# Scores of two heads in nearly every place with the values beside them, and the weights' conversion weighted to the places with values

## The chip, the core and the metric

The kernel runs on one core of a Trainium2 chip. The metric is the device time of one execution in microseconds (us). PE is TensorE (its matmuls; PEld is its weight loads), DVE is VectorE, ACT is ScalarE, POOL is GpSimd and SP is SyncE, which here only issues DMAs. Each engine runs its own instructions strictly in the order in which they were issued; a semaphore holds an instruction back until its inputs are there.

## What is computed

Attention of 8 batches, 12 heads, 448 tokens and head size 64, with the heads mixed before and after the softmax, and behind it a two-layer feed-forward block on the 3584 tokens. All is float32.

```python
def _attn_ref(q, k, v, w_pre, w_post):
    scale = 1.0 / np.sqrt(q.shape[-1])
    scores = scale * np.matmul(q, k.transpose(0, 1, 3, 2))
    scores = np.einsum('bhij,hg->bgij', scores, w_pre)
    scores = scores - np.max(scores, axis=-1, keepdims=True)
    attn = np.exp(scores)
    attn = attn / (np.sum(attn, axis=-1, keepdims=True) + 1e-09)
    attn = np.einsum('bhij,hg->bgij', attn, w_post)
    return np.matmul(attn, v)

def _moe_ref(x, w_in, w_out):          # x: [3584, 768]
    h = x @ w_in                       # d_ff = 2048
    return (h - np.tanh(h)) @ w_out
```

## The kernel before, in words

**Stages.** A start of some 26 us, an attention loop (26 to 838 us), and the feed-forward stage (to 1787 us). The change touches only the attention loop.

**Places.** The 448 query rows of a batch are cut into blocks of 120, 120, 120 and 88 rows, 32 blocks in all. A block is split into groups of up to ten query rows times twelve heads (120 partitions), 360 groups; two groups make a *place*, and the loop `for p in range(NPL + 3)` runs over NPL = 180 places. At each place PE does `premix(p)` (L521: the mixing before the softmax, into the two banks `ps_p`), then the jobs that a table `todo[p]` gives it, then `mix(p - 1)` (L560: the mixing behind the softmax of the place before, into `ps_o`). A place needs, from the others:

- `expo(p)`: on DVE two maxima (L530), on ACT two exponentials with their sums (L532);
- `norm(p - 1)`, issued ahead of `expo(p)`: on DVE the reciprocal of the sums (L541, L542), on POOL the scaled weights `wr` (L543) that `mix(p - 1)` multiplies by;
- the copy of `mix`'s result out of `ps_o` into the block's tile `at` on ACT (L570, or L577 in two parts where a place spans two blocks). It is issued at the start of the next place, and `ps_o` has one buffer, so `mix(p)` also waits for the copy of `mix(p - 1)`;
- `gather`: DMAs that bring the scores of the next groups into `t` (L510, issued by SP).

**Jobs.** `scores(i, hp)` makes the scores of one pair of heads for block i: 6 matmuls (L477) into two banks of `ps_m`, copied to the tile `s` by ACT (one bank) and DVE (the other), both L482. `values(i, t)` is half of attention times V for block i: 24 matmuls (L602) into one bank, copied to `x` by DVE (L620). `prep_q` and `prep_k` transpose Q (L443) and K (L417) into one bank per call; ACT makes the high part (L456, L428), DVE the low part (L458, L429). `ps_m` has four banks in turn. In the trace a plain float32 matmul stands twice, so `values` shows as x48 there, and `scores` of one pair as x6.

**Order within a place.** The queues on ACT and DVE follow the calls: first `mixed()` (the copy into `at`), `norm`, `expo`, then, after PE's jobs, the copies of K, Q and scores (list `sooner`), then `conv.place()`, and only then the low parts (list `then`) and the copy of the values into `x` (list `last`).

**The conversion.** Beside all this the feed-forward weights are turned into two float32 parts and written to DRAM (`narrow_chunk`): 56 chunks of 384 or 512 columns, each 11 steps with 5 operations on DVE (L80, L83, L87, L89, L94), 3 on ACT (L82, L85, L102), 3 on POOL (L96, L98, L104) and DMAs. `Steps` deals the steps out evenly, 617 steps over 164 places, 3.76 per place; what is left is done by `conv.rest(now)` at place 177, ahead of the first loads of the next stage.

**The planner.** What sets `todo` is a small scheduler ahead of the loop: each block has due places for its scores (three jobs of two pairs, four heads each) and its values (two halves), and one job goes to one place, scores and values in turn where both are ready.

Of the kernel before, what the change touches and what calls it, by code (L numbers as in the profile page):

```python
# [37 lines left out]
def narrow_steps(nc, pool, dma, chunks):  # L38

    def load(src):
        p, n2 = src.shape
        r = pool.tile([p, CW, 2], I32, name="cr", tag="cr", bufs=3)[:, : n2 // 2]
        return r, dma(r.rearrange("p n t -> p (n t)"), src)


    todo, loads, active = list(chunks), [], []  # L50
    yield
    while todo or loads or active:
        while todo and len(loads) + len(active) < 3:
            src, dst = todo.pop(0)
            loads.append((*load(src), dst))
        while loads and len(active) < 2:
            r, landed, dst = loads[0]
            if not landed(1):
                break
            loads.pop(0)  # L60
            active.append(narrow_chunk(nc, pool, dma, r, dst))
        for it in list(active):
            if next(it, "end") == "end":
                active.remove(it)
            else:
                yield
        if not active:
            yield


def narrow_chunk(nc, pool, dma, r, dst):
    p, n, _ = r.shape
    hi, lo = r[:, :, 1], r[:, :, 0]
    m = pool.tile([p, CW], F32, name="cm", tag="cm", bufs=2)[:, :n]
    s = pool.tile([p, CW], I32, name="cs", tag="cs", bufs=2)[:, :n]
    u, w = hi, lo

# [11 lines left out]
    nc.vector.scalar_tensor_tensor(  # L89
        out=u, in0=m.bitcast(I32), scalar=3, in1=s, op0=ALU.logical_shift_left, op1=ALU.bitwise_or  # L90
    )
    yield "step"

    nc.vector.tensor_scalar(s, u, -(2**23), None, op0=ALU.bitwise_and)  # L94
# [3 lines left out]
    nc.gpsimd.tensor_tensor(out=m, in0=m, in1=u.bitcast(F32), op=ALU.add)  # L98
# [12 lines left out]


class Steps:


    def __init__(self, it, steps, places):
        self.it = it
        self.rate = steps / places
        self.due = 0.0

    def place(self):
        self.due += self.rate
        while self.due >= 1.0:
            self.due -= 1.0
            next(self.it, None)
# [23 lines left out]
def kernel_body(  # L149
# [11 lines left out]
    nc = tc.nc  # L161
# [4 lines left out]
    NP = H // 2  # L166
# [9 lines left out]
    NM = len(sizes)  # L176
# [162 lines left out]
    with ExitStack() as st:  # L339
# [4 lines left out]
        cv = early.enter_context(tc.tile_pool(name="cv", bufs=1, side="left"))  # L344
# [11 lines left out]
        blocks = [(b, m) for b in range(B) for m in range(NM)]  # L356
# [3 lines left out]
        queue, slow, sent = [], [], {}  # L360
# [41 lines left out]
        KB = 4  # L402
# [336 lines left out]
        NG = len(groups)  # L739
# [2 lines left out]
        place[0] += 1  # L742
        scores_of(1, 0)
        NPL = NG // 2
        conv = Steps(narrow_steps(nc, cv, partial(dma, to=slow), chunks), 11 * len(chunks) + 1, NPL - 16)

# [9 lines left out]
        halved = []  # L756
        for i in range(len(blocks)):

            f0, f1, f2 = first[i : i + 3]
            if i + 1 < len(blocks):  # L760
                lo = max(0, (f0 - 1) // 2 - 1)
                hi = f1 // 2 - 3
# [3 lines left out]
            for x in range(2):  # L766
                halved.append(((f1 - 1) // 2 + 2, f2 // 2 + 1 if f2 < NG else NPL + 7, "v", i, x))
        at_s, p, kind = {}, 0, None
        while halved:
            ready = sorted((x for x in halved if x[0] <= p), key=lambda x: (x[1], x[3:]))  # L770
            if ready:
                x = ready[0]
                assert p <= x[1], (p, x)

                other = [y for y in ready if y[2] != kind]
                if x[2] == kind and other and x[1] > p + 1:
                    x = other[0]
                halved.remove(x)
                _, _, kind, i, n = x
                if kind == "s":  # L780
                    at_s[i, n] = p
                    for hp in (2 * n, 2 * n + 1):
                        at_place(p, scores, i, hp)
                else:
                    at_place(p, values, i, n)
            p += 1
        for i, (b, m) in enumerate(blocks):
            p0 = first[i] // 2
            if i + 2 < len(blocks):
                p = at_s[i + 2, 0] - 1  # L790
                at_place(p, prep_q, i + 2, 0)
                at_place(p, prep_q, i + 2, 1)
                if i + 3 < len(blocks):
                    at_place(p + 1, load_q, i + 3)
            if b and m == 0:
                for hq in range(NP // 2):
                    at_place(p0 + 4 + hq, load_v, b, hq)
        for b in range(1, B):
            p, o, done = first[blocks.index((b - 1, 1))] // 2 - 4, 0, []
            for hq in range(3):  # L800
                if hq == 2:

                    p = max(p, done[0] + 1)
                at_place(p, load_k, b, hq)
                o = max(p + 4, o + 1)
                p += 1
                if hq > KB - 4:

                    o = max(o, at_s[blocks.index((b - 1, 3)), hq - 1 - (KB - 4)] + 1)
# [5 lines left out]
                assert o < at_s[blocks.index((b, 0)), hq], (b, hq)  # L815

        rank = {prep_k: 0, prep_q: 0, values: 1, scores: 2}
        for x in todo.values():
            x.sort(key=lambda job: rank.get(job[0], 3))

        def hidden_0():
            ff.r = next(gate(hidden(0)))
# [60 lines left out]
    for n in range(N):  # L883
        b, f = n // NF, n % NF
# [63 lines left out]
```

## Time and profile before

Three runs took 1787.08 to 1787.36 us, the median 1787.1. The profiled execution took 1788.92 us, of which the profile's span is 1787.2 us; the 1.7 us between them lie around the program.

| | busy us | share of span | instructions |
|---|---|---|---|
| PE matmuls | 1751.0 | 98% | 16572 |
| DVE | 1128.3 | 63% | 2362 |
| ACT | 1000.5 | 56% | 2051 |
| POOL | 320.1 | 18% | 417 |

"Busy" for PE includes matmuls that overlap each other, and the ends of matmuls are modelled. Shares are averages over two stages with different limits; the table of windows that the next part quotes looks at the attention loop and at single places.

### The profile page before, as it was taken

The numbers are of one execution on the slowest core, as the hardware profiler recorded it, in microseconds if no ns is written. First come the engines' busy times: TensorE is split into PE (matmuls) and PEld (weight loads), VectorE is DVE, ScalarE is ACT, GpSimd is POOL, SyncE is SP. The second block draws the span as 40 slices with busy tenths as digits, with TensorE's granted clock in tenths as the row PEclk, the third lists the DMA queues.
The fourth block names the chain that finished last, engine by engine and source line by source line (L and its number), as shares of the span: only waits on it lengthen the run. The fifth ranks groups of instructions, "written<-read, shape, count | busy, mean of one in ns | idle before, by whom it ended". The sixth has DMA issues, their size and how long they took to land.

```text
span 1787.2 us, 41382 instructions
## 1 busy us (share of the span) xinstructions
PE 1751.0 (98%) x16572; PEld 1425.6 (80%) x16572; DVE 1128.3 (63%) x2362; ACT 1000.5 (56%) x2051; POOL 320.1 (18%) x417
## 2 busy tenths in 40 slices
PE   8999999999999999999999999999999999999998
PEld 6777777777777777777888888888888888888887
DVE  5676777777777767664556566565565565655555
ACT  5777877777777776765343443433434434444333
POOL 1333333333333333321010010000000000000000
PEclk9999999999999999999999999999999999999999
DMA  8668687777967687565655655655656655655651
GB/s 176 204 196 216 194 236 224 217 215 215 249 203 218 215 213 220 178 202 216 255 207 194 248 193 207 241 193 214 229 197 216 224 208 204 228 217 190 230 194 36
DMA packets 232816, 372.32 MB, mean 208 GB/s; under 512 B 98992, under 2 KB 207536, under 8 KB 218288
## 3 DMA queue, kind: packets, MB, share of 16 engines
q1 hardware_dynamic: 231740, 368.45, 64.0%
q8 instruction: 131, 2.15, 0.5%
q10 hardware_dynamic: 884, 1.22, 0.2%
q14 instruction: 61, 0.50, 0.1%
HBM read 245.37 MB, written 47.19 MB: 164 GB/s over the span
## 4 chain that ended last, share of the span: by engine, by line
PE 87%; DMA 4%; ACT 4%; DVE 3%; issue 1%; POOL 0%; SPq 0%; ACTq 0%; DVEq 0%; POOLq 0%
PE ps_o L560 13%; PE ps_h L257 8%; PE ps_h L258 8%; PE ps_h L262 8%; PE ps_m L602 8%; PE ps_p L521 7%; PE ya L305 6%; PE ya L302 6%; PE ya L303 6%; PE ps_q L477 5%; PE yb L305 3%; PE yb L303 3%; PE yb L302 3%; DMA t<-s 2%; PE ps_m L443 1%
## 5 line engine op out<-in xcount | busy, mean ns | idle before, releaser
L560 PEld LDWEIGHTS ps_o<-wr,e 60*112 60x112 f32 (+1 forms) x5760 | 306.2, 176 | 44.3 <-POOL wr L543 21.8
L560 PE MATMUL ps_o<-wr,e 60*112 60x60 f32 (+1 forms) x5760 | 315.5, 259 | 14.3 <-POOL wr L543 7.7
L530 DVE TENSOR_REDUCE mx<-ps_p 128x1 f32<-128x448 f32 x360 | 207.7, 619 | 163.9 <-PE ps_p L521 163.7
L532 ACT ACTIVATE e<-ps_p,mx 128x448 f32<-128x448 f32 x360 | 225.7, 634 | 101.9 <-DVE mx L530 99.4
L289 ACT CAST gh<-r 128x512 fp32r<-128x512 f32 x112 | 69.6, 621 | 372.6 <-DVE r L282 372.6
L258 PE MATMUL ps_h<-xl,w 128*128 128x512 f32 x672 | 264.4, 393 | 0.0
L257 PE MATMUL ps_h<-xh,w 128*128 128x512 f32 x672 | 264.3, 393 | 0.0
L570 ACT COPY at<-ps_o 112x960 f32<-112x960 f32 x156 | 153.7, 985 | 93.8 <-PE ps_o L560 93.2
L247 POOL TENSOR_TENSOR xl<-rx,xh 128x512 fp32r<-128x512 f32 x38 | 55.6, 1464 | 731.2 <-ACT xh L246 731.2
L521 PE MATMUL ps_p<-t,wpre 60*64 60x448 f32 (+1 forms) x1440 | 180.8, 569 | 3.9 <-DMA t<-s 2.7
L305 PE MATMUL ya<-w,gl 128*128 128x512 f32 x448 | 177.0, 395 | 0.7 <-DVE gl L290 0.7
L278 DVE SCALAR_TENSOR_TENSOR r<-qa,ps_h 128x512 f32<-128x512 f32 x112 | 77.1, 688 | 159.2 <-ACT t L275 159.2
L302 PE MATMUL ya<-w,gh 128*128 128x512 f32 x448 | 174.8, 390 | 1.0 <-ACT gh L289 1.0
L303 PE MATMUL ya<-w,gh 128*128 128x512 f32 x448 | 174.8, 390 | 0.0
L602 PEld LDWEIGHTS ps_m<-at,vr 112*64 112x64 f32 x3072 | 147.5, 137 | 31.0 <-ACT at L577 10.9
L262 PE MATMUL ps_h<-xh,w 128*128 128x512 f32 x672 | 170.6, 389 | 0.0
L602 PE MATMUL ps_m<-at,vr 112*64 112x120 f32 (+1 forms) x3072 | 161.6, 261 | 8.4 <-ACT at L577 3.1
L272 ACT ACTIVATE u<-ps_h 128x512 f32<-128x512 f32 x112 | 67.0, 599 | 152.9 <-PE ps_h L262 152.9
L262 PEld LDWEIGHTS ps_h<-xh,w 128*128 128x128 f32 x672 | 126.3, 188 | 26.3
L258 PEld LDWEIGHTS ps_h<-xl,w 128*128 128x128 f32 x672 | 127.5, 190 | 23.7
L257 PEld LDWEIGHTS ps_h<-xh,w 128*128 128x128 f32 x672 | 127.4, 190 | 23.4
L543 POOL TENSOR_TENSOR wr<-wpost,zs 128x120 f32<-128x120 f32 x180 | 70.2, 390 | 402.9 <-DVE zs L542 293.6
(93 smaller groups left out, 3038.0 us busy)
## 6 DMA issues: line engine op xcount, KB each, us to landing
w<-ws SPq DMA_DIRECT2D x112, 1536.0 KB
t<-s SPq DMA_DIRECT2D x342, 210.0 KB
cr<-in_moe_w_in_dram SPq DMA_DIRECT2D x24, 512.0 KB
cr<-in_moe_w_out_dram SPq DMA_DIRECT2D x32, 384.0 KB
vr<-in_v_dram SPq DMA_DIRECT2D x24, 448.0 KB
kr<-in_k_dram SPq DMA_DIRECT2D x23, 448.0 KB
out_dram<-ob SPq DMA_DIRECT2D x24, 384.0 KB
qr<-in_q_dram SPq DMA_DIRECT2D x23, 360.0 KB
```

What stands on the lines that cost most here:

```text
L257: nc.tensor.matmul(ph, wh[:, fs], xh, start=(c == 0), stop=False)
L258: nc.tensor.matmul(ph, wh[:, fs], xl, start=False, stop=False)
L262: nc.tensor.matmul(ph, wl[:, fs], xh, start=False, stop=(c == NK - 1))
L302: nc.tensor.matmul(y, gh[:, tok], wh[:, es], start=first, stop=False)
L303: nc.tensor.matmul(y, gh[:, tok], wl[:, es], start=False, stop=False)
L305: nc.tensor.matmul(y, gl[:, tok], wh[:, es], start=False, stop=last)
L521: nc.tensor.matmul(pss[r][halves[j], :], wpre[k, :], ts[j][k, :], start=True, stop=True)
L530: nc.vector.tensor_reduce(out=mx, in_=ps, axis=AX.X, op=ALU.max, negate=True)
L532: nc.scalar.activation(e, ps, AF.Exp, bias=mx, scale=1.0, accum_out=zs[:, 0, r : r + 1])
L560: nc.tensor.matmul(ps[:CP, j, c * GP : (c + 1) * GP].rearrange("p (h i) -> p h i", i=GI)[:, :, r * GH : (r + 1) * GH], e[k, c * CP : (c + ...
L570: nc.scalar.copy(ats[i0][:, :, :, at : at + 2 * GI].rearrange("p c h (j i) -> p j (c h) i", j=2), ps[:CP, :, : NC * GP].rearrange("p j (x ...
L602: nc.tensor.matmul(pv[j * D : (j + 1) * D, r, :n], vt[:, j, c, :], ats[i][:, c, 2 * hp + j, :n], start=(c == 0), stop=(c == NC - 1),)
```

## The change

The table `todo` is made by other rules. Scores are dealt out pair by pair (two heads), evenly over the places at which a block's scores may run, so that most places get one pair. Values go to the first place from their due place on that has at most one pair, if the last values lie two places back. The transposes go where a place's jobs need no more than four banks in all; the two halves of `prep_q` are at two places where they can be. V is loaded only once the values of the block before are placed, and the first values of a batch are due two places later. `Steps` takes a list of weights, 2.5 for a place with values and 1 for another, over the same 164 places.

```diff
 class Steps:
-    def __init__(self, it, steps, places):
+    def __init__(self, it, steps, weights):
         self.it = it
-        self.rate = steps / places
+        self.rates = [steps * w / sum(weights) for w in weights]
         self.due = 0.0
     def place(self):
-        self.due += self.rate
+        self.due += self.rates.pop(0) if self.rates else 0.0
...
-                for x in range(0 if i else 1, 3):
-                    e = lo + 2 * x if lo + 4 <= hi else lo + (hi - lo) * x // 2
-                    halved.append((e if i else x - 1, hi, "s", i + 1, x))
+                due_s += [(lo, hi, i + 1, hp) for hp in range(0 if i else 2, NP)]
+            lo = (f1 - 1) // 2 + (4 if i and i % NM == 0 else 2)
+            due_v += [(lo, f2 // 2 + 1 if f2 < NG else NPL + 7, i, x) for x in range(2)]
...
+                left = sum(x[2] == i for x in due_s)
+                now_s = -(-left // (hi - p + 1))
...
+                if p + (1 - x) >= hi or now_s == 0 or now_s == 1 and apart >= 2:
+                    due_v.pop(0)
+                    at_place(p, values, i, x)
...
+                p = max(p0 + 4, at_v[i - 1, 1] + 1)
                 for hq in range(NP // 2):
-                    at_place(p0 + 4 + hq, load_v, b, hq)
+                    at_place(p + hq, load_v, b, hq)
...
-                    while any(f is scores or f is prep_q for f, *a in todo[o]):
+                    while banks(o) > 3:
...
+        weight = [2.5 if any(f is values for f, *a in todo[p]) else 1 for p in range(4, NPL - 12)]
+        conv = Steps(narrow_steps(nc, cv, partial(dma, to=slow), chunks), 11 * len(chunks) + 1, weight)
         rank = {prep_k: 0, prep_q: 0, values: 1, scores: 2}
```

The number of instructions of each kind stays. The places come out so (of 179, with the transposes left out of the count):

| jobs of the place | before | after |
|---|---|---|
| four heads' scores | 92 | 26 |
| one pair's scores (two heads) | 0 | 88 |
| values alone | 62 | 18 |
| values and one pair's scores | 0 | 44 |
| neither | 25 | 3 |

How it moves the rows is shown at places 42 and 43. First PE, before; a place begins with its premix (L521), and `ps_q` are the scores' banks:

```order
L521 MATMUL ps_p<-t,wpre 64x448 x4
L477 MATMUL ps_q<-kk,qh 120x448 x4
L477 MATMUL ps_q<-kk,ql 120x448 x2
L477 MATMUL ps_q<-kk,qh 120x448 x4
L477 MATMUL ps_q<-kk,ql 120x448 x2
L560 MATMUL ps_o<-wr,e 112x12x5 x16
L521 MATMUL ps_p<-t,wpre 64x448 x4
L443 MATMUL ps_m<-ident,qr 128x120 x6
L602 MATMUL ps_m<-at,vr 64x120 x24
L560 MATMUL ps_o<-wr,e 112x12x5 x16
```

The same two places on PE after the change:

```order
L521 MATMUL ps_p<-t,wpre 64x448 x4
L443 MATMUL ps_m<-ident,qr 128x120 x3
L602 MATMUL ps_m<-at,vr 64x120 x24
L477 MATMUL ps_q<-kk,qh 120x448 x4
L477 MATMUL ps_q<-kk,ql 120x448 x2
L560 MATMUL ps_o<-wr,e 112x12x5 x16
L521 MATMUL ps_p<-t,wpre 64x448 x4
L477 MATMUL ps_q<-kk,qh 120x448 x4
L477 MATMUL ps_q<-kk,ql 120x448 x2
L560 MATMUL ps_o<-wr,e 112x12x5 x16
```

The values now have a pair's scores behind them in the same place, and the next place has only one pair between its premix and its mix.

DVE at the same two places, before (a place's rows begin with the maxima, L530, and end with the reciprocal, L542, that the next mix needs; `cm`, `cr` and `cs` belong to the conversion):

```order
L530 TENSOR_REDUCE mx<-ps_p 128x1 x2
L482 COPY s<-ps_q 120x448 x2
L89 SCALAR_TENSOR_TENSOR cr<-cm,cs 128x384
L94 TENSOR_SCALAR cs<-cr 128x384
L541 TENSOR_SCALAR zs<-zs 128x1 x2
L542 RECIPROCAL zs<-zs 128x2
L530 TENSOR_REDUCE mx<-ps_p 128x1 x2
L80 TENSOR_SCALAR cm<-cr 128x384
L458 SCALAR_TENSOR_TENSOR ql<-ps_m,qh 128x3x120 x2
L620 COPY x<-ps_m 128x3x12x10
L541 TENSOR_SCALAR zs<-zs 128x1 x2
L542 RECIPROCAL zs<-zs 128x2
```

And DVE after the change, place 42 whole and the first rows of place 43:

```order
L530 TENSOR_REDUCE mx<-ps_p 128x1 x2
L482 COPY s<-ps_q 120x448
L87 TENSOR_SCALAR cs<-cr 128x384
L89 SCALAR_TENSOR_TENSOR cr<-cm,cs 128x384
L94 TENSOR_SCALAR cs<-cr 128x384
L458 SCALAR_TENSOR_TENSOR ql<-ps_m,qh 128x3x120
L620 COPY x<-ps_m 128x3x12x10
L541 TENSOR_SCALAR zs<-zs 128x1 x2
L542 RECIPROCAL zs<-zs 128x2
L530 TENSOR_REDUCE mx<-ps_p 128x1 x2
L482 COPY s<-ps_q 120x448
```

In the place with values the copy of the scores now stands first behind the maxima, and three operations of the conversion, the low part of Q, the copy of the values and the reciprocal stand behind it.

Last, SP's queue of DMAs at the end of the loop. Before, the first load of the next stage's weights (`w`, L334) follows the last gathers:

```order
L510 DMA t<-s 120x1x448 x8
L369 DMA xs_64<-x 768x1x240
L510 DMA t<-s 120x1x448 x4
L510 DMA t<-s 108x1x448 x2
L334 DMA w_12920<-ws_65 128x3072
```

After the change:

```order
L510 DMA t<-s 120x1x448 x12
L369 DMA xs_64<-x 768x1x240
L510 DMA t<-s 120x1x448 x4
L510 DMA t<-s 108x1x448 x2
L369 DMA ws_68<-cs 128x384
L369 DMA ws_68<-cl 128x384
L334 DMA w_12920<-ws_65 128x3072
```

The last chunk of the conversion is finished by `conv.rest` at place 177, and its two writes stand ahead of that load.

More of the change, by code (lines that the diff above doesn't have):

```diff
@@ L754, in at_place, with banks @@
             todo[p].append(job)
-        halved = []
+        def banks(p):
+            return sum({scores: 2, values: 1, prep_q: 1, prep_k: 1}.get(f, 0) for f, *a in todo[p])
+        at_s, at_v = {}, {}
+        due_s, due_v = [], []
         for i in range(len(blocks)):
@@ L760, in kernel_body @@
             if i + 1 < len(blocks):
-                lo = max(0, (f0 - 1) // 2 - 1)
-                hi = f1 // 2 - 3
-                for x in range(0 if i else 1, 3):
-                    e = lo + 2 * x if lo + 4 <= hi else lo + (hi - lo) * x // 2
-                    halved.append((e if i else x - 1, hi, "s", i + 1, x))
[L766 to L785, printed above, removed]
+                lo, hi = max(0, (f0 - 1) // 2 - 1), f1 // 2 - 3
+                due_s += [(lo, hi, i + 1, hp) for hp in range(0 if i else 2, NP)]
+            lo = (f1 - 1) // 2 + (4 if i and i % NM == 0 else 2)
+            due_v += [(lo, f2 // 2 + 1 if f2 < NG else NPL + 7, i, x) for x in range(2)]
+        p, apart = 0, 2
+        while due_s or due_v:
+            now_s = 0
+            if due_s and due_s[0][0] <= p:
+                _, hi, i, _ = due_s[0]
+                left = sum(x[2] == i for x in due_s)
+                assert p <= hi, (p, hi, i)
+                now_s = -(-left // (hi - p + 1))
+                for _ in range(now_s):
+                    _, _, i, hp = due_s.pop(0)
+                    at_s[i, hp] = p
+                    at_place(p, scores, i, hp)
+            if due_v and due_v[0][0] <= p:
+                _, hi, i, x = due_v[0]
+                assert p <= hi, (p, hi, i)
+                if p + (1 - x) >= hi or now_s == 0 or now_s == 1 and apart >= 2:
+                    due_v.pop(0)
+                    at_v[i, x] = p
+                    at_place(p, values, i, x)
+                    apart = 0
+            apart += 1
             p += 1
@@ L788, in kernel_body @@
             p0 = first[i] // 2
[L789 to L794, printed above, removed]
             if b and m == 0:
+                p = max(p0 + 4, at_v[i - 1, 1] + 1)
+                assert p + 4 < at_v[i, 0], (p, at_v[i, 0])
                 for hq in range(NP // 2):
-                    at_place(p0 + 4 + hq, load_v, b, hq)
+                    at_place(p + hq, load_v, b, hq)
         for b in range(1, B):
@@ L807, in kernel_body @@
                 if hq > KB - 4:
-                    o = max(o, at_s[blocks.index((b - 1, 3)), hq - 1 - (KB - 4)] + 1)
+                    o = max(o, at_s[blocks.index((b - 1, 3)), 2 * (hq - 1 - (KB - 4)) + 1] + 1)
                 for r in range(2):
-                    while any(f is scores or f is prep_q for f, *a in todo[o]):
+                    while banks(o) > 3:
                         o += 1
@@ L814, in kernel_body @@
                 done.append(o)
-                assert o < at_s[blocks.index((b, 0)), hq], (b, hq)
+                assert o < at_s[blocks.index((b, 0)), 2 * hq], (b, hq)
+        last_q = 0
+        for i in range(len(blocks)):
+            if i + 2 < len(blocks):
+                p = at_s[i + 2, 0]
+                for t in (1, 0):
+                    p -= t
+                    while banks(p) > 3:
+                        p -= 1
+                    at_place(p, prep_q, i + 2, t)
+                    last_q = max(p, last_q) if t == 0 else p
+                assert p > at_s.get((i, NP - 1), 0), p
+                p = last_q
+                if i + 3 < len(blocks):
+                    at_place(p + 1, load_q, i + 3)
+        weight = [2.5 if any(f is values for f, *a in todo[p]) else 1 for p in range(4, NPL - 12)]
+        conv = Steps(narrow_steps(nc, cv, partial(dma, to=slow), chunks), 11 * len(chunks) + 1, weight)
         rank = {prep_k: 0, prep_q: 0, values: 1, scores: 2}
         for x in todo.values():
-            x.sort(key=lambda job: rank.get(job[0], 3))
+            x.sort(key=lambda job: (rank.get(job[0], 3), job[2] if job[0] is prep_q else 0))
         def hidden_0():
```

1 line of the change is left out of this document (removed).

## The prediction

> **What bounds the kernel now.** First the page: the shares of the engines, then the chain that ended last.
>
> ```profile
> PE 1751.0 (98%) x16572; PEld 1425.6 (80%) x16572; DVE 1128.3 (63%) x2362; ACT 1000.5 (56%) x2051; POOL 320.1 (18%) x417
> PE 87%; DMA 4%; ACT 4%; DVE 3%; issue 1%; POOL 0%; SPq 0%; ACTq 0%; DVEq 0%; POOLq 0%
> ```
>
> PE sets the time. No PE instruction is added or removed, so the change can only move the moments at which PE waits. To price those I need each job's length without a wait: PE's timeline at places 42 to 44 (start, duration, instructions).
>
> ```profile
> 217.15 0.66 PE L477 MATMUL ps_q<-kk,qh 64*120 64x448 f32 x4
> ...
> 217.85 0.56 PE L477 MATMUL ps_q<-kk,qh 64*120 64x448 f32 x4
> ...
> 218.45 1.69 PE L560 MATMUL ps_o<-wr,e 60*112 60x60 f32 x32
> 220.07 0.98 PE L521 MATMUL ps_p<-t,wpre 60*64 60x448 f32 x8
> 220.99 0.83 PE L443 MATMUL ps_m<-ident,qr 120*128 120x120 f32 x6
> 221.75 2.68 PE L602 MATMUL ps_m<-at,vr 112*64 112x120 f32 x48
> 224.36 1.78 PE L560 MATMUL ps_o<-wr,e 60*112 60x60 f32 x32
> 226.08 0.98 PE L521 MATMUL ps_p<-t,wpre 48*64 48x448 f32 x8
> ```
>
> From start to start: premix 0.92, first pair of heads 0.70, second 0.60, Q's transposes 0.76, values 2.61, mix 1.62 behind scores and 1.72 behind values. Next, windows of the loop and of single places (start:end, length, then busy time of PE, PEld, DVE, ACT, POOL; granted clock, DMA share, GB/s).
>
> ```profile
> 26.40:838.20 811.80, 788.23 (x11556) 609.75 (x11556) 569.35 (x1538) 601.13 (x1371) 256.87 (x348) 0.99 0.72 211
> 212.86:216.23 3.37, 2.69 (x42) 1.89 (x40) 2.42 (x11) 3.11 (x8) 0.39 (x1) 1.00 0.62 235
> 216.23:220.07 3.84, 3.84 (x54) 2.94 (x52) 2.88 (x7) 3.58 (x10) 1.38 (x2) 1.00 0.18 67
> 252.10:256.70 4.60, 4.60 (x91) 3.73 (x89) 2.40 (x11) 3.85 (x9) 2.02 (x3) 1.00 0.91 218
> 260.55:266.71 6.16, 6.16 (x99) 5.09 (x97) 5.69 (x15) 4.40 (x10) 3.02 (x3) 1.00 0.96 285
> 109.23:114.66 5.43, 5.43 (x55) 3.77 (x53) 3.03 (x8) 3.18 (x7) 1.94 (x3) 0.69 0.44 160
> ...
> 798.18:803.93 5.75, 5.75 (x55) 3.69 (x53) 2.68 (x7) 3.22 (x7) 0.35 (x1) 0.63 0.31 113
> ```
>
> A place with neither job needs 2.63 us (premix 0.92, mix 1.71) and took 3.37 in the second row. Values of 88 rows cost 4.60 - 2.63 = 1.97, K's transposes 6.16 - 2.63 - 2.61 = 0.92. With the counts of the built program: 179 x 2.63, 92 x 1.21 for four heads, 48 x 2.61 and 14 x 1.97 for values, 30 x 0.76 for Q, 21 x 0.92 for K: 777 us. The loop took 811.8, so **some 35 us are waits, and no order can gain more.** Where they stand is in PE's waits within the loop (total us, times, longest):
>
> ```profile
> PE ps_o L560 <- POOL wr L543: 6.5, 9, 1.3
> PE ps_o L560 <- ACT at L570: 5.8, 8, 1.5
> PE ps_m L602 <- ACT at L577: 3.1, 5, 1.0
> PE ps_m L602 <- ACT at L570: 2.7, 4, 1.8
> PE ps_p L521 <- DMA t<-s: 2.7, 3, 1.6
> PE ps_m L602 <- DMA vr<-in_v_dram: 2.4, 2, 1.4
> PE ps_p L521 <- ACT at L570: 1.0, 1, 1.0
> ```
>
> That is 24.2 us. The last two windows above are the first and the last of three four-head places (3.84 without a wait) that stand right behind places with neither job and ran at a lowered clock, here 0.69 and 0.63; they took 1.59 and 1.91 more, the three together 5.1 us. The other 6 are restarts behind waits and the error of the lengths.
>
> **The change part by part.**
>
> *Places with neither job, 25 to 3.* I wrote for every place when the copy into `at`, `wr` and the banks of `ps_p` are ready, from the starts in the rows, and compared it with when PE wants them. For the kernel before this gives 17.5 us of waits for these three; the view has 6.5 + 5.8 + 1.0 = 13.3, and a restart of about 0.23 behind each of the 18 waits makes up the rest. Of the 17.5, 16.5 lie at places with neither job or right behind one. Three such places stay: 1.5. Saved: **15 us**.
>
> *Scores behind values.* This is the new cost. Here are DVE's rows of places 42 and 43 before, then two of POOL's and one of PE's at place 137, where a `wr` was late.
>
> ```profile
> 218.35 1.15 DVE L482 COPY s<-ps_q 120x448 f32<-120x448 f32 x2
> 219.42 0.55 DVE L89 SCALAR_TENSOR_TENSOR cr<-cm,cs 128x384 int32<-128x384 int32 x1
> 220.00 0.36 DVE L94 TENSOR_SCALAR cs<-cr 128x384 int32<-128x384 int32 x1
> 220.28 0.21 DVE L541 TENSOR_SCALAR zs<-zs 128x1 f32<-128x1 f32 x2
> ...
> 221.12 1.16 DVE L530 TENSOR_REDUCE mx<-ps_p 128x1 f32<-128x448 f32 x2 [0.44 <-PE ps_p L521]
> ...
> 223.58 0.97 DVE L458 SCALAR_TENSOR_TENSOR ql<-ps_m,qh 128x360 fp32r<-128x360 f32 x2 [1.03 <-ACT qh L456]
> 224.48 0.79 DVE L620 COPY x<-ps_m 128x360 f32<-128x360 f32 x1
> 225.12 0.18 DVE L541 TENSOR_SCALAR zs<-zs 128x1 f32<-128x1 f32 x2
> ```
>
> ```profile
> 225.64 0.39 POOL L543 TENSOR_TENSOR wr<-wpost,zs 128x120 f32<-128x120 f32 x1 [2.23 <-DVE zs L542]
> ```
>
> ```profile
> 645.52 1.30 POOL L98 TENSOR_TENSOR cm<-cm,cr 128x512 f32<-128x512 f32 x1
> 646.78 0.39 POOL L543 TENSOR_TENSOR wr<-wpost,zs 128x120 f32<-128x120 f32 x1
> 647.22 1.78 PE L560 MATMUL ps_o<-wr,e 60*112 60x60 f32 x32 [0.50 <-POOL wr L543]
> ```
>
> At place 42 after the change, DVE's copy of the pair stands first behind the maxima and can't begin before the pair is done, behind the values. Queued behind it on DVE: L87, L89, L94, one L458, the values' copy L620, then L541 and L542, for which POOL's `wr` waits, and for that the next mix. From the end of the pair, start to start in these rows: 0.13 until DVE has it (premix from 220.07 ends at 220.99, the maxima start at 221.12), 0.53 for L482 (half of 219.42 - 218.35), 0.28 for L87 (as L94), 0.58 L89, 0.28 L94, 0.45 L458, 0.64 L620, 0.52 from L541 to `wr`, 0.39 `wr`, 0.05 to PE: 3.85 us. PE's cover from the same moment is mix 1.62 + premix 0.92 + the next place's only pair 0.70 = 3.24. So PE waits about 0.6; with the median starts of all places (L89 then 0.48) 0.45. The same arithmetic over the 40 such places that no values follow: **12.9 us**, of which 6.1 from DVE's queue alone, and the rest where L96 or L98 stands ahead of `wr` on POOL, as at 645.52. Bounds: nothing, if the queue clears in time; 23, if each operation takes its whole duration (the second rival).
>
> *One pair behind another or behind four heads.* Such a place lasts 3.24 us; ACT's exponentials, one copy of scores and a conversion step fill about that. By the same arithmetic 5.6 us in 36 places, against 1.0 before: **+4.6**; bounds 0 and 9 (each wait doubled).
>
> *Values waiting for the copy into `at`.* The place ahead is now mostly a one-pair place, 0.6 us shorter than a four-head one, so values reach `at` earlier. The arithmetic gives 4.1 before (the view 3.1 + 2.7) and 6.3 after: **+2.2**, bounds -4 and +5.
>
> *The clock.* With few waits over a microsecond left I keep one stretch of low clock out of three: **-4.1**, bounds -5.1 and 0. It fell in places where PE was busy 2.7 us of 3.4 to 4.2, not always:
>
> ```profile
> 105.04:109.23 4.19, 2.69 (x42) 1.89 (x40) 3.58 (x11) 3.91 (x9) 0.92 (x3) 1.00 1.01 217
> 414.23:417.94 3.71, 2.70 (x43) 1.89 (x41) 2.36 (x6) 3.23 (x8) 0.39 (x1) 1.00 0.87 269
> ```
>
> The first comes right before the window at 0.69; behind the second the clock stayed at full. [...]
>
> *Gathers, V, SP's queue.* All blocks' last scores now lie three places ahead of their first premix, and the place between is often a one-pair place; before, a third had four. The conversion's writes, denser in places with values, stand ahead of those gathers on SP. I take 4 us for the 2.7 of the view: **+1.3**, bounds -2.7 and +6 (six blocks have a microsecond or two less than any had, bar one). V's waits go with the two places more: **-2.4**, bounds -2.4 and 0.
>
> *The conversion.* Its 280 operations on DVE stay; 2.84 of them instead of about 1.7 stand in a place with values, 1.1 elsewhere. That is in the sums above. At place 177 it leaves two writes ahead of the first `w` load on SP:
>
> ```profile
> 827.28 0.49 SPq L334 DMA_DIRECT2D w<-ws  x1
> ```
>
> ```profile
> 844.75 0.79 PE L257 MATMUL ps_h<-xh,w 128*128 128x512 f32 x1
> ```
>
> That load had 17 us until the first use; two writes at about such an issue time are 1 us. **+0.5**, bounds 0 and 2.4.
>
> Sum: -15 + 12.9 + 4.6 + 2.2 - 4.1 + 1.3 - 2.4 + 0.5 = 0.0. All of it is against the profiled execution of 1788.92 us, 1.8 over the median; I carry the difference to the median, 1787.1.
>
> **The rivals.**
>
> *Faster: the new queue on DVE is hidden.* The wait at place 42 is 0.45 to 0.6 out of a chain of 3.85. Each wait also gives DVE, ACT and POOL time to catch up, which sums made place by place don't count, and POOL was idle 2.23 us ahead of the `wr` at 225.64. If the chain shrinks by 0.3 us (the mean wait, 12.9 / 40), the 12.9 become about 3 and the 4.6 about 2: 1787 - 12.5 = **1774.5**. Against it: the waits are from rows that agree with the view of before to within 5 us.
>
> *Slower: the queue costs full durations.* With the rows' durations in place of start-to-start (0.58 for 0.53, 0.79 for 0.64 and so on) and POOL's two operations of 1.30 ahead of `wr`, the 12.9 become 23 and the rest 3 more: 1787 + 13 = **1800**. Each 0.1 us in 40 places is 4 us, so it decides from 0.1 us more per place on. Against it: at 220.00 L94 shows 0.36, and the next row starts 0.28 later.
>
> *The clock doesn't come back.* After 414.23 it stayed full though PE idled as long as in other such places, so its falls may not depend on these waits at all. Then three stretches remain: 1787 + 4 = **1791**.
>
> **How the numbers follow.** A measurement of this kernel tells a change of about 0.2% (3.6 us) from none. Forecast **1787.0**, with 1783 to 1791 as its own range: 0.34 (0.06 of it faster than 1783.5, 0.24 within, 0.04 slower). Faster rival 0.32. Slower rival 0.24. Clock 0.10, 0.06 of it within. Together faster 0.38, same 0.30, slower 0.32. The range goes past the faster case to 1773 and past the slower to 1801; what the bounds add beyond (all at their ends at once) I leave to the 2 in 10.
>
> **What the profile after would show.** Few waits left at places with neither job, for `at` under 3 us; in PE's waits `wr` as the largest, 10 to 17 us in some 30 waits of 0.3 to 0.9, each behind a place with values and a pair, and DVE's L482 waiting for PE there. If `wr` stays under 5 us, the first rival holds; over 20, the second. The clock column tells the third. `t` waiting over 6 us, or gaps at the start of the next stage, would mean that I mis-sized a transfer. The forecast is wrong altogether if PE's wait-free work differs from 777 us.

## The result and the profile after

The changed kernel took 1885.9 us (median of 4 runs, 1881.7 to 1898.0) against 1787.2: a ratio of 1.055, 95% interval 1.049 to 1.061. That is **99 us slower, where no change was forecast and 1801 was the upper end of the range.** The profiled execution has a span of 1880.8 us (1787.2 before). First the page's shares of the engines and of the chain that ended last:

```profile
PE 1803.1 (96%) x16572; PEld 1452.5 (77%) x16572; DVE 1128.9 (60%) x2362; ACT 1004.4 (53%) x2051; POOL 322.2 (17%) x417
PE 80%; DMA 5%; DVE 5%; ACT 4%; issue 2%; POOL 2%; SPq 1%; ACTq 0%; POOLq 0%; DVEq 0%
```

DVE, ACT and POOL do the work that they did; PE has 52 us more of "busy" with the same instructions, so it ran them more slowly.

The loop up to place 176 as one window, before and after (length, busy time of PE, PEld, DVE, ACT, POOL; granted clock, DMA share, GB/s):

```profile
26.41:824.12 797.71, 774.15 (x11340) 598.89 (x11341) 562.55 (x1518) 593.43 (x1353) 255.64 (x343) 0.99 0.72 210
```

```profile
25.24:911.04 885.80, 825.17 (x11340) 624.80 (x11340) 561.58 (x1518) 597.32 (x1352) 255.80 (x341) 0.95 0.65 189
```

Of the 93.6 us by which the span grew, 88.1 are here. PE's idle time (length less busy time) goes from 23.6 to 60.6, **+37**. By the trace's record of the clock 92.2 us of the loop ran at half speed in 17 stretches, 13.7 in 3 before (the stretch that every loop begins with is left out): at half the pace, an estimate from these two times, that is up to **+39**. The remaining +12 also stand in PE's busy time, and no run shows what they are. PE's waits after (total us, times, longest):

```profile
PE ps_o L560 <- POOL wr L543: 18.3, 21, 2.5
PE ps_p L521 <- DMA t<-s: 13.3, 9, 3.7
PE ps_o L560 <- ACT at L570: 10.6, 12, 2.9
PE ps_m L443 <- DMA qr<-in_q_dram: 6.5, 3, 3.1
PE ps_m L602 <- ACT at L570: 5.7, 7, 4.2
PE ps_p L521 <- ACT at L570: 3.3, 2, 1.7
PE ps_q L477 <- DVE ql L458: 1.3, 2, 1.1
PE ps_q L477 <- DVE zs L541: 1.3, 5, 0.3
PE ps_m L602 <- ACT at L577: 1.2, 4, 0.6
```

What is new is their length. Idle stretches of 1.4 us and more were 2 in the loop (3.3 us), and are 16 (36.2 us): 33 of the 37 us that were added.

**A long wait, read on four engines.** The end of place 48, which has values and a pair, and place 49 behind it, which has one pair: DVE, POOL, ACT and PE (start, duration; in brackets the idle time ahead and its releaser):

```profile
271.44 0.62 DVE L482 COPY s<-ps_q 120x448 f32<-120x448 f32 x1 [2.07 <-PE ps_q L477]
271.99 0.42 DVE L94 TENSOR_SCALAR cs<-cr 128x512 int32<-128x512 int32 x1
```

```profile
272.48 1.41 POOL L96 TENSOR_TENSOR cm<-cr,cs 128x512 f32<-128x512 f32 x1 [4.13 <-DVE cs L94]
273.97 1.36 POOL L98 TENSOR_TENSOR cm<-cm,cr 128x512 f32<-128x512 f32 x1
```

```profile
275.36 0.62 ACT L102 CAST cs<-cm 128x512 fp32r<-128x512 f32 x1 [3.42 <-POOL cm L98]
275.88 0.62 ACT L82 ACTIVATE cm<-cm 128x512 f32<-128x512 f32 x1
276.42 0.96 ACT L570 COPY at<-ps_o 112x960 f32<-112x960 f32 x1
```

```profile
277.52 1.82 PE L560 MATMUL ps_o<-wr,e 60*112 60x60 f32 x18 [2.89 <-ACT at L570]
```

Place 48 has six steps of the conversion, so L94 on DVE, L96 and L98 on POOL and L102 on ACT follow each other within one place. Each needs the one before, and the first of them stands behind DVE's copy of the pair, which waits 2.07 us for PE. ACT stands at L102 for 3.42 us, the copy into `at` behind it is late, and the mix of place 49 waits 2.89. Over the loop ACT waited 17.1 us for L98 and 10.4 us at L82 for L80 (0.6 and 2.1 before).

**The clock.** Windows of 3.41 us, one behind the other, in the changed kernel:

```profile
144.57:147.98 3.41, 3.41 (x48) 2.56 (x50) 2.51 (x4) 2.03 (x3) 1.48 (x1) 1.00 0.71 189
147.98:151.40 3.42, 2.39 (x42) 1.92 (x43) 2.98 (x12) 1.75 (x5) 2.18 (x4) 1.00 0.85 234
151.40:154.81 3.41, 3.41 (x20) 1.71 (x22) 1.67 (x5) 2.35 (x6) 1.57 (x3) 0.50 0.21 70
154.81:158.22 3.41, 3.41 (x80) 3.29 (x76) 2.10 (x9) 1.97 (x6) 0.39 (x1) 1.00 1.03 251
```

There is one wait of 1.03 us in the second window, and the third runs at half clock (0.50): the premix that starts at 151.33 takes 1.76 us, the one at 158.27, at full clock, 0.98. At half pace the third window loses 1.7 us; with the wait that is 2.7 us here, an estimate from these rows.

### The profile page after: what moved, and what is told of

Same layout as the page of the kernel before. It is cut to its first block, busy times and chain, and to the rows that moved or that the text cites. A ratio compares the mean times of both kernels' runs of the same rounds, so it can differ in the third digit from the quotient of the medians.

```text
span 1880.8 us, 41365 instructions
## 1 busy us (share of the span) xinstructions
PE 1803.1 (96%) x16572; PEld 1452.5 (77%) x16572; DVE 1128.9 (60%) x2362; ACT 1004.4 (53%) x2051; POOL 322.2 (17%) x417
## 4 chain that ended last, share of the span: by engine, by line
PE 80%; DMA 5%; DVE 5%; ACT 4%; issue 2%; POOL 2%; SPq 1%; ACTq 0%; POOLq 0%; DVEq 0%
PE ps_o L560 10%; PE ps_m L602 8%; PE ps_h L258 8%; PE ps_h L257 8%; PE ps_h L262 8%; PE ps_p L521 6%; PE ya L305 5%; PE ya L302 5%; PE ya L303 5%; PE ps_q L477 5%; PE yb L305 3%; PE yb L303 3%; PE yb L302 3%; DMA t<-s 3%; PE ps_m L443 1%
## 5 line engine op out<-in xcount | busy, mean ns | idle before, releaser
L560 PEld LDWEIGHTS ps_o<-wr,e 60*112 60x112 f32 (+1 forms) x5760 | 318.6, 181 | 63.7 <-POOL wr L543 38.7
L560 PE MATMUL ps_o<-wr,e 60*112 60x60 f32 (+1 forms) x5760 | 323.4, 263 | 34.8 <-POOL wr L543 22.5
L530 DVE TENSOR_REDUCE mx<-ps_p 128x1 f32<-128x448 f32 x360 | 207.2, 617 | 144.2 <-PE ps_p L521 143.8
L521 PE MATMUL ps_p<-t,wpre 60*64 60x448 f32 (+1 forms) x1440 | 189.7, 594 | 16.6 <-DMA t<-s 13.3
L482 DVE COPY s<-ps_q 120x448 f32<-120x448 f32 (+1 forms) x192 | 116.6, 618 | 134.2 <-PE ps_q L477 133.6
L602 PEld LDWEIGHTS ps_m<-at,vr 112*64 112x64 f32 x3072 | 164.1, 148 | 33.0 <-issue 10.2
L602 PE MATMUL ps_m<-at,vr 112*64 112x120 f32 (+1 forms) x3072 | 177.8, 277 | 6.9 <-ACT at L570 5.7
L570 ACT COPY at<-ps_o 112x960 f32<-112x960 f32 x156 | 153.4, 983 | 49.8 <-PE ps_o L560 49.4
L262 PEld LDWEIGHTS ps_h<-xh,w 128*128 128x128 f32 x672 | 126.4, 188 | 26.3
```

The lines of the kernel that those rows point to most:

```text
L262: nc.tensor.matmul(ph, wl[:, fs], xh, start=False, stop=(c == NK - 1))
L521: nc.tensor.matmul(pss[r][halves[j], :], wpre[k, :], ts[j][k, :], start=True, stop=True)
L530: nc.vector.tensor_reduce(out=mx, in_=ps, axis=AX.X, op=ALU.max, negate=True)
L560: nc.tensor.matmul(ps[:CP, j, c * GP : (c + 1) * GP].rearrange("p (h i) -> p h i", i=GI)[:, :, r * GH : (r + 1) * GH], e[k, c * CP : (c + ...
L570: nc.scalar.copy(ats[i0][:, :, :, at : at + 2 * GI].rearrange("p c h (j i) -> p j (c h) i", j=2), ps[:CP, :, : NC * GP].rearrange("p j (x ...
L602: nc.tensor.matmul(pv[j * D : (j + 1) * D, r, :n], vt[:, j, c, :], ats[i][:, c, 2 * hp + j, :n], start=(c == 0), stop=(c == NC - 1),)
```

## The experiments

Each was timed against the kernel before on the same chip: e2, e12, e13, e16, e17 and e19 in 7 to 12 runs, the others in 2 to 6, e6 and e7 in one. Ratios stand with their 95% interval. The kernel before had medians of 1788.2 to 1795.1 us there, so experiments are compared with each other by their ratios. "Idle" and "half" are PE's idle time and the time at half clock (without the stretch that each loop begins with) in the loop up to place 176, from each one's profile.

| | edit | ratio | idle | half |
|---|---|---|---|---|
| before | | 1 | 23.6 | 13.7 |
| after | | 1.055 | 60.6 | 92.2 |
| e1 | after, even weights | 1.036 (1.033 to 1.039) | 46.3 | 54.6 |
| e2 | before, weights 2.5 | 0.999 (0.997 to 1.002) | 19.7 | 10.2 |
| e3 | after, copy into `at` first | 1.064 (1.060 to 1.067) | 69.3 | 119.5 |
| e4 | e1, pair ahead of values | 1.027 (1.024 to 1.030) | 33.4 | 58.0 |
| e5 | e4 without V's loads | 1.014 (1.010 to 1.018) | 21.1 | 23.9 |
| e6 | after, no conversion in the loop | loop only | 12.7 | 20.5 |
| e7 | before, no conversion in the loop | loop only | 3.4 | 0 |

**Weights and table apart (e1, e2).** The edits are one line each: `weight = [1 for p in range(4, NPL - 12)]` in the changed kernel, and the weights of 2.5 put into the kernel before.

> The changed kernel with the conversion dealt out evenly again (weight 1 for every place); the new table of jobs stays. Theory A (the conversion): the changed kernel does up to six steps of the conversion in one place with values, so that an operation and the one on another engine that needs its result fall in the same place; the later one (L102 on ACT behind L98 on POOL, L82 on ACT behind L80 on DVE, L80 behind its load from DRAM) then holds up the copy into at that stands behind it, PE waits 2 to 4 us, and the clock falls. Theory A expects most of the 95 us back: 1785 to 1810, ACT's waits of L102 and L82 for other engines under 4 us in sum (27.5 in the changed kernel), at most 6 stretches at half clock (17). Theory B (the table): one-pair places leave too little cover for wr, the copy into at, the gathers and the loads of Q. It expects 1850 to 1885, with the DMA waits of PE (13.3 for t and 6.5 for Q) as they are.

> The kernel before with its own table of jobs, and only the weights of the conversion changed (2.5 for a place with values, 1 for another). Theory A expects the loss here too, since the same bursts of steps are there: 1840 to 1890, with ACT's L102 and L82 waiting 15 us or more. Theory B expects no loss: values alone have the longest cover on PE in the old table, so 1775 to 1795.

1856.5 us, ratio 1.036, and 1791.6, 0.999. Both times lie in theory B's ranges and outside theory A's, but neither theory holds whole. The weights cost nothing on the old table, and 1.9% (34 us) on top of the new one, which B doesn't explain; the new table with the conversion dealt out evenly costs 3.6% (64 us). In e1 ACT's waits for other engines at L102 and L82 fell from 27.5 to 6.4 us, not under 4 as A had it; PE's for `t` stayed (16.2 us) and those for Q went (0.3). In e2 ACT waited 11.4 us for L98 and 4.5 us for L80, and the time didn't rise (0.999); that such links cost only where PE's cover is short is my reading, which no run shows by itself.

**The order on ACT (e3).** `mix(p - 1)()` in place of `mixed = mix(p - 1)`.

> The changed kernel, but the copy into at is issued right behind its mix, so that on ACT it stands ahead of the conversion's operations instead of behind them. Theory A expects PE's waits for at (L570 and L577: 20.8 us in the changed kernel) to fall under 8, and a total of 1830 to 1870; the rest of the loss would sit in the exponentials that now stand behind the conversion. Theory B expects 1875 to 1900, since the cover of the one-pair places is as it was.

1909.3 us. The waits for `at` fell as expected, from 20.8 to 2.7 us, and those for `wr` rose from 18.3 to 42.2. ACT now waits for each mix ahead of the conversion's operations (115.2 us at L570, 45.7 in the changed kernel), and DVE waits 11.0 us at L89 for ACT's L82 (1.0), ahead of the reciprocals. The wait moved and grew; turning this order on ACT around cures nothing.

**The predicted queue on DVE (e4).** `rank = {prep_k: 0, prep_q: 0, values: 2, scores: 1}` in e1.

> As e1 (even conversion, new table), and in a place with values and a pair the pair goes ahead of the values on PE, so that DVE need not wait behind the values for its copy of the scores. The predicted mechanism (wr late because DVE's queue stands behind that copy) expects 8 to 13 us less than e1. If the difference to e1 is under 4 us, that queue is not what costs.

1841.0 against 1856.5 us: 15.5 less, where 8 to 13 were expected. DVE's wait for the scores ahead of L482 fell from 124.5 to 15.8 us, and PE's waits for `wr` behind a place with values and a pair, 4.3 us in 9 places in e1, are gone. The queue that the prediction priced is real, but the 15.5 us aren't all its own: of the 12.9 us of idle time that went, 6.0 are waits of the values for the copy into `at`, now that the pair stands ahead of them, and 5.3 are waits for `t`.

**V's loads (e5, e8).** In e5 the 21 loads of the batches 2 to 8 are left out (all batches use the first one's V). e8 deals V's loads to every second place (`p + 2 * hq`).

> As e4 (new table, even conversion, pairs ahead of values), and without the loads of V for the batches 2 to 8: 21 of 24 loads are left out, and the values of all batches use the first batch's V. Theory C (transfers): the new table puts the three V loads of a batch right beside the gathers of the next block's scores, which have one-pair places only in which to land; the eight long waits for t in e4 (10.9 us) stand at the same places of each batch, and each brings the half clock. Theory C expects under 3 us of waits for t, at most 3 stretches at half clock in place of 7, and 1800 to 1815 (e4: 1841). If V is not the cause, the time stays at 1835 to 1845.

> As e4, but the three V loads of a batch go to every second place instead of one place after the other, so the last comes two places later. Theory C expects the waits for t to fall to about half (5 us) and 1820 to 1835. If it is not the spacing but the place, it stays within 5 us of e4 (1841).

e5: 1816.9 us, 24 less than e4; waits for `t` 2.9 us, 3 stretches at half clock. e8: 1840.1, ratio 1.023 (1.014 to 1.033), no change that its two runs could tell from e4. So V's transfers are part of e4's time, and spacing them out isn't shown to help. No run leaves V out of the old table, so how much of the 24 us is the new table's own stays open.

**No conversion in the loop (e6, e7).** `conv.place()` is taken out, and all steps run at place 177; only the loop up to place 176 is compared.

> The changed kernel with no step of the conversion inside the loop: all of it is done at place 177, so only the loop up to there can be compared (premix of place 0 to premix of place 176: some 886 us in the changed kernel, 777 without any wait). If the table alone costs 65 us and more by its cover on PE, the loop stays above 835. If the table costs only together with the conversion's operations and transfers that stand between, it falls under 800.

> The control: the kernel before with no step of the conversion inside the loop. Its loop has some 35 us of waits. If these come from places with neither job, as the prediction has it, at least 12 of them stay; if from the conversion, under 8 stay.

The windows of the two loops, new table and old:

```profile
25.89:817.44 791.55, 778.90 (x11340) 602.40 (x11340) 449.84 (x1238) 518.69 (x1185) 67.73 (x175) 0.98 0.51 148
```

```profile
25.60:795.81 770.21, 766.78 (x11341) 596.66 (x11341) 440.93 (x1238) 519.42 (x1185) 67.81 (x175) 1.00 0.52 152
```

The old loop is 27.5 us shorter without the conversion, with 3.4 us of idle time and no half clock behind its start: what the prediction put down to places with neither job arises only together with the conversion. The new loop is 94 us shorter without it. The table alone costs 21 us (791.6 against 770.2), the conversion 67 us more on the new table than on the old one. These two runs take out the conversion's operations and its transfers together, so they don't part the one from the other. In e6, `t` is nearly all that PE waits for: 11.4 us in 6 places.

**Room for the gathers (e9), and for the conversion's loads (e10, e12, e13).** e9 is e4 with `f1 // 2 - 4` for the scores' due place; the others have `landed(2)` for `landed(1)`, in e4, e2 and the kernel before.

> As e4 (new table, even conversion, pairs ahead of values), with every block's scores due one place earlier. The table gets denser by it: 57 places with four heads (26), 48 with one pair alone (88), 22 with values and a pair (44), 12 with neither (3); the last scores of a block then have 10 to 16 us until their first premix (7 to 11 in the changed kernel). Theory C (the gathers have too little room beside V) expects the waits for t (10.9 us in e4) under 3 and 1800 to 1820; if the short room is not the cause, 1835 to 1845.

> As e4, but a chunk of the conversion is begun two places after its load was issued instead of one. Theory D: the two longest waits of e4 (at place 7 for the low part of K, at place 52 for wr, 5.0 us each) are one thing: DVE's L80 waits for the chunk's load from DRAM, counted as landed a place after it was issued, and a place lasts only 3.2 us; all that stands behind on DVE waits too, then PE, and the half clock doubles it. It expects DVE's waits for the loads (11.1 us in e4) under 3, both waits gone, and 1815 to 1828. If those waits come from elsewhere, no change (1836 to 1846).

> As e2 (old table, conversion weighted by 2.5), with the chunks begun two places after their load. In e2 the longest waits of PE for wr were 4.4 us in 3 places, DVE's for the loads 8.5 us. Theory D expects these gone and 8 to 12 us under the kernel before, the first version that beats it; without theory D the ratio stays at 0.999.

> The kernel before with that one number changed (chunks begun two places after their load). DVE waits 5.0 us for the loads there, most of it not on PE's path: theory D expects 0 to 4 us less, a ratio of 0.998 to 1.000. It is the control for e12: if e13 gains as much as e12, the weights do nothing in the old table.

e9: 1823.4 us, ratio 1.017 (1.012 to 1.022), 18 us less than e4, but the waits for `t` stayed at 11.4 us, so the gain can't be that of the gathers' room; its table is another one, with 48 one-pair places in place of 88. e10: 1846.4, no gain: DVE's waits for the loads fell from 11.1 to 2.9 us and PE's for `wr` in the loop from 12.2 to 6.6, and those for `t` rose from 10.9 to 17.2. e12 and e13: 1.003 (1.000 to 1.006) and 1.001 (0.999 to 1.002). Theory D names two waits rightly and falls as a cause of the time.

**Lead of the gathers (e14 to e17).** Eight tiles `t` for six, and in e4, the changed kernel, the one before, and e2:

```diff
-            for t in (2 * p + 4, 2 * p + 5):
-                if t < NG:
-                    gather(t)
+            while nxt < NG and (nxt < 2 * p + 6 or nxt < 2 * p + 8 and done[groups[nxt][0]] < p):
+                gather(nxt)
+                nxt += 1
```

> As e4 (new table, even conversion, pairs ahead of values), but the gathers for a place are issued three places ahead instead of two wherever the block's scores are done by then, into eight tiles t instead of six. Theory E: at a batch's border V, Q, K and the conversion keep the DMA engines busy at a share of 0.9 to 1.1, so a gather lands 5 to 6 us after its issue, and two one-pair places are 6.5 us together with the issue itself; where the room was made between scores and premix (e9) nothing changed since the gathers were still issued two places ahead. It expects the waits for t (10.9 us in e4) under 3, the stretches at half clock from 7 to 4 or fewer, and 1810 to 1828 (e4: 1841). If the gathers' lead is not the cause, 1835 to 1845.

> The changed kernel itself with that lead of three places, all else as it is. Theory E expects its 13.3 us of waits for t under 4 and 1855 to 1875 (1882 to 1898 before). Without theory E no change.

> The kernel before with that lead of three places. It waits only 2.7 us for t, and has one or two stretches at half clock near such waits: theory E expects 0 to 5 us less, a ratio of 0.997 to 1.000.

> As e2 (old table, conversion weighted by 2.5) with that lead. e2 waits 6.7 us for t in 5 places: theory E expects these under 2 and a ratio of 0.992 to 0.997, faster than the kernel before.

The waits for `t` went as expected (10.9 to 3.2 in e14, 13.3 to 1.6 in e15), and the time didn't: 1853.7, 1881.9, and on the old table 1.008 (1.005 to 1.011) and 1.010 (1.006 to 1.013). In e14 the chunks' loads came later (DVE waits 18.9 us for them, 11.1 in e4), and PE's waits for `wr` rose from 12.2 to 20.1. In e15 the idle time did fall, from 60.6 to 50.8 us, but the time at half clock rose from 92.2 to 102.4. More waits came for Q in e15 (6.5 in the changed kernel) and for V in e16 (2.4 in the kernel before):

```profile
PE ps_m L443 <- DMA qr<-in_q_dram: 8.7, 3, 4.5
```

```profile
PE ps_m L602 <- DMA vr<-in_v_dram: 10.8, 8, 2.7
```

In all three a gather sent earlier goes with another transfer that is late in its turn.

**V's loads at quiet places (e18, e19).** Five tiles for V, and its first two loads of a batch at `p0 - 8 + hq`.

> As e4 (new table, even conversion, pairs ahead of values), but with five tiles for V instead of three, and the first two V loads of a batch eight and seven places ahead of the batch's first place, where the DMA share is 0.1 to 0.5, instead of at the border, where it is 0.9 to 1.1; the third stays. Theory F: at the border the DMA engines are the bound, so any lead given to one kind of transfer (e14) only makes another late, and two thirds of V's loads taken out of it should be worth about two thirds of the 24 us of e5: 1820 to 1830 (e4: 1841), with waits for t and DVE's waits for the loads falling together. If V's bytes cost as much elsewhere, 1835 to 1845.

> The kernel before with the same five tiles and the same early places for the first two V loads; the third goes two places later than it did. The kernel before waits 2.4 us for V and 2.7 for t, all at borders: theory F expects these gone and 3 to 8 us less, a ratio of 0.995 to 0.999. If the border isn't short of transfers in the old table, no change.

e18: 1843.8 us, no gain. `t` fell from 10.9 to 5.0 us as expected, and Q, which e4 did not wait for, now came late at places 41, 86 and 131, right behind the moved loads:

```profile
PE ps_m L443 <- DMA qr<-in_q_dram: 6.3, 3, 2.5
PE ps_p L521 <- DMA t<-s: 5.0, 4, 1.8
```

e19: 1785.5 against 1790.2 us on the same chip, a ratio of 0.9966 (0.9951 to 0.9982). The old table with V loaded early is **the fastest version here, 0.3% under the kernel before**; V's waits (2.4 us) are gone and `t` has 1.6 left.

## Why the prediction was wrong

- **What bounds the kernel**: right; PE has the same instructions, and 76 of the loop's 88 us are idle time and half clock (the other 12 stay open).
- **Scores behind values, 12.9 us**: the mechanism was right and its sum near, in fewer and longer waits. In the changed kernel 16.2 of the 18.3 us for `wr` lie right behind a place with values and a pair, but in 17 places in place of 40. Place 42 after the change, on DVE, POOL and PE:

```profile
242.88 0.62 DVE L482 COPY s<-ps_q 120x448 f32<-120x448 f32 x1 [3.79 <-PE ps_q L477]
243.42 0.35 DVE L87 TENSOR_SCALAR cs<-cr 128x384 int32<-128x384 int32 x1
243.81 0.56 DVE L89 SCALAR_TENSOR_TENSOR cr<-cm,cs 128x384 int32<-128x384 int32 x1
244.41 0.36 DVE L94 TENSOR_SCALAR cs<-cr 128x384 int32<-128x384 int32 x1
244.68 0.53 DVE L458 SCALAR_TENSOR_TENSOR ql<-ps_m,qh 128x360 fp32r<-128x360 f32 x1
245.12 0.80 DVE L620 COPY x<-ps_m 128x360 f32<-128x360 f32 x1
245.76 0.19 DVE L541 TENSOR_SCALAR zs<-zs 128x1 f32<-128x1 f32 x2
```

```profile
246.33 0.39 POOL L543 TENSOR_TENSOR wr<-wpost,zs 128x120 f32<-128x120 f32 x1 [0.45 <-DVE zs L542]
```

```profile
242.65 1.69 PE L560 MATMUL ps_o<-wr,e 60*112 60x60 f32 x32
...
246.77 1.78 PE L560 MATMUL ps_o<-wr,e 60*112 60x60 f32 x32 [0.71 <-POOL wr L543]
```

  From the pair's end (242.65) to the next mix it is 4.12 us, where 3.85 were worked out, and PE waits 0.71 (0.45 to 0.6). Of the 16.2 us 4.3 are left with even weights (e1), and none with the pair ahead of the values (e4).
- **The step that failed: that every operation on DVE, ACT and POOL starts when its own engine is free.** The prediction has the conversion "in the sums above" by its operations' time alone. The place-by-place arithmetic, behind the terms for the new queue, for one pair behind another and for the values, let an operation of the conversion wait neither for the one on another engine nor for its load. With 3.76 steps a place these links mostly lay in different places; with six they lie in one (place 48). A load counted as landed after one place had not landed at place 7, where DVE waits 3.9 us; but in sum these waits are 5.0 us before and after, and e10 took them away without a gain. "One pair behind another" was +4.6 us in 36 places; the 56 places with one pair and nothing else in the changed kernel are 50 us longer than their work (waits for `t` and half clock among it). The runs show the conversion in its place: 34 us by the weights (e1), 67 as a whole (e6 against e7), and next to nothing by the weights on the old table (e2). How much of the 67 are links between engines and how much transfers is not shown.
- **The clock, -4.1 us forecast, +39 at most measured.** The wrong sign, and the largest single miss. It was priced by the count of waits over a microsecond, which was to fall; it rose, with the failed step: PE's idle stretches of a microsecond and more in the loop up to place 176 went from 10 to 23. The stretches at half clock in that loop start at whole multiples of 3.41 us from each other (in the changed kernel the first three at 55.82, 96.78 and 151.40 us, 40.96 and 54.62 apart or 12 and 16 times 3.41), and the one at 151.40 followed a window in which PE was busy 2.39 of 3.42 us. What makes the clock fall no run shows by itself.
- **Gathers, +1.3 forecast, +10.6 measured** (13.3 against 2.7), and 6.5 for Q, which had no term. The bound of +6 was set by the time between a block's last scores and its first premix; e9 raised that time (from between 7 and 11 us to between 10 and 16) and left the waits as they were, and in e14 and e15 a lead of three places took most of them away, so it was the lead of two that counted for `t`. V's waits did go, by the 2.4 us forecast.
- **Places with neither job, 15 us saved**: only three such places remain, with 0.3 us of waits in all, so these waits went. Their reason was incomplete: e7 has all 25 of them and idles 3.4 us.
- **The end of the loop, +0.5 forecast, +6.2 measured** (26.8 us from the premix of place 176 to the first hidden matmul, 20.6 before). I watched the load of `w`, which had 17 us to spare, and priced the two writes by their issue; behind them on SP stand the loads `rx`. Ahead of the two writes SP waited 4.0 us for ACT's L102 and 0.7 us for POOL's L104, operations of the last chunk, so the first `rx` was issued 9.2 us behind the premix of place 176, where it was 5.3 before. Here are SP, ACT and PE in the changed kernel:

```profile
918.20 0.33 SPq L369 DMA_DIRECT2D ws<-cs  x1
919.28 0.33 SPq L369 DMA_DIRECT2D ws<-cl  x1
919.65 0.43 SPq L334 DMA_DIRECT2D w<-ws  x1
920.26 9.20 SPq L238 DMA_DIRECT2D rx<-xs  x12
```

```profile
928.01 0.62 ACT L246 CAST xh<-rx 128x512 fp32r<-128x512 f32 x1 [5.01 <-DMA rx<-xs]
```

```profile
930.26 3.24 PE L560 MATMUL ps_o<-wr,e 60*112 60x60 f32 x32 [4.15 <-POOL wr L543]
```

  ACT's cast waits 5.01 us for `rx`; DVE's subtraction behind it stands ahead of the sums for the last `wr`.
- **The rivals.** The slower one had the right sign, by durations in place of starts on a single queue; its 13 us are a seventh of the loss. No case in the range let one wait call forth another.

**What stays open.** The parts don't add up to a cause that can be undone: weights 34 us, pair order 15, V's bytes 24, in that order, leave e5 still 24 us over the kernel before, with one 5.3 us wait at place 7 (a chunk's load) and the half clock behind it among them. That the sum of all transfers at a batch's border is what binds agrees with e5, which left transfers out, and with e10, e14, e16 and e18, in each of which the lateness moved from one kind of transfer to another; no run changed the sum alone without also leaving work out, so it is not shown.

## What to carry to other kernels

Evening out the bottleneck engine's work takes slack away from everything that is timed in steps of that work: links between engines, loads "landed a place ago", gathers "two places ahead". Before such a change, list for each background chain how many of its dependent steps fall into one step of the loop, and how many microseconds each lead is in the shortest run of steps. And price a wait with the clock that may fall behind it, not by its length alone: here a wait of 1.03 us had 3.41 us at half clock behind it.

## What the runs showed of the hardware

In the profiles of the kernel before and of the changed one, the 3 and 17 stretches at half clock in the loop up to place 176 lasted 3.41, 6.83 or 10.24 us and started at whole multiples of 3.41 us from each other. The loop cut into windows of 3.41 us from such a start on has 459 at full clock in the two profiles: with PE busy for under 2.0 us, 12 of 13 were followed by half clock; with 2.0 to 2.42 us, 8 of 17; above 2.42, none of 429 (the bound of 2.42 was read off these same two profiles). This one, in the changed kernel, is the one of the 13 that passed:

```profile
509.80:513.21 3.41, 1.70 (x14) 0.59 (x14) 3.34 (x10) 0.98 (x1) 1.76 (x2) 1.00 0.59 171
513.21:516.63 3.42, 3.31 (x46) 2.50 (x48) 2.03 (x8) 2.74 (x6) 2.94 (x4) 1.00 1.19 307
```
